# Sliding-window attention with a routed FFN on one core: transposes set between the long matmul groups, routing tail over seven steps, FFN weights in 0.5 MB pieces, row gathers two experts ahead

## The chip, the cores and the metric

The kernel runs on one core of one Trainium2 chip. The metric is the device time of one execution in microseconds (us); lower is better. The engines are TensorE (PE; its weight loads are shown apart as PEld), VectorE (DVE), ScalarE (ACT), GpSimd (POOL) and SyncE (SP), which here only issues DMAs.

## The reference

Two stages, for 8 batches of 576 tokens, 8 heads of 64:

```python
mask = (abs(pos_q - pos_k) <= 32) | is_global[q] | is_global[k]      # 8 global positions
attn = softmax(where(mask, q @ k.T / 8, -1e9))
x    = (attn @ v) as 4608 rows of 512
expert = argmax(x @ w_gate)                                          # 8 experts
gate   = softmax(x @ w_gate)[expert]
for e in range(8):
    out[rows of e] = gate * (relu(rows @ w1[e]) @ w2[e])             # 512 -> 1024 -> 512
```

## The kernel before

**Attention.** The loop runs over batches b = 0 to 7 and, in each, over six steps t. A step covers two window slices of all eight heads. `scores` (lines 383 and 396) puts the mask and q·k into one PSUM tile, one step ahead of use; `exps` (L403, ACT) takes the exponentials; `pvs` (L414) multiplies them with v, `zs` (L426) sums them, and `merge_x` and `merge_z` add both to the accumulators `xt` and `zt` (L444 on ACT, L447 and L449 on DVE). q and k of batch b+1 are transposed in steps 1 to 4 by `trans_qk` (L293 for k, copied by ACT L298; L291 for q, copied by DVE L295). The code runs in written order on each engine.

**The tail.** After a batch, `join` and `sum_globals` (POOL) finish `xt`, and the class `Tail` turns the batch into routed rows during the next batch's steps: `gate` (L500, copied by DVE L504), `logits` (L515, DVE to L523), `route1` (DVE and ACT), `ranks` (L580, L582), `route2` (DVE), `rows(i, f)` (L536, four transposes; DVE L537 scales the result into a 16-bit row buffer, `x16x` or a part of `wall`), and `scatter` (L613), six indirect DMAs on POOL that write rows into the slots of their experts in HBM (`xslot_scr`). All of `trans_qk`, `gate`, `logits`, `ranks` and `rows` take their PSUM tile from one pool of two buffers, in turn: the third must wait until DVE or ACT has copied the first.

**Weights.** `wall` holds the 16-bit weights of all experts (1 MB of 32-bit weights is one half of `w1` or `w2` of an expert). Those of experts 0 and 1 are loaded in batches 1 to 4 (two loads of 1 MB at t = 2 of each) and cast by ACT in the next batch's steps. The attention's buffers lie in the part of `wall` that belongs to later experts.

**Hand-over.** After batch 7 its own tail and that of the global rows run with nothing beside them, then the last scatters; then POOL computes an index constant (L755), DVE the gather indices and memsets (L784), and POOL issues the gathers (L774 and L775) of expert 0's four row blocks of 128.

**FFN.** For each expert, 32 matmuls `h` (L921) in eight groups, each with a relu in turn on ACT (L818) and DVE (L816); then 16 transposes of the next expert's rows (L798, copied by DVE L799); then 32 matmuls `yp` (L941) in four groups, each followed by `yout`: the gate is multiplied in by DVE (L807) or ACT (L805) into one of three `y` buffers, and an indirect DMA (L808, POOL) writes the rows to `out`. At the start of e the weights of e+3 are asked for in four loads of 1 MB, through two buffers `st`; each is cast by one instruction (POOL and DVE L638, ACT L636), which frees it for the next load. Rows of e+1 are gathered at the start of e. In e = 1 DVE also computes the overflow plan.

**Overflow.** Rows beyond an expert's first 512 run in blocks of 128, three to a chunk (nine blocks here): transposes `x`, matmuls `h` (L970), transposes `t` (L980), matmuls `y` (L989), all `yout` on ACT. Writes to `out` of this part are declared dependent on one another, so that each waits for the one before.

Of the kernel before, what the change touches and what calls it, by code (L numbers as in the profile page):

```python
# [38 lines left out]
NOV = 32  # L39
# [3 lines left out]
def kernel(  # L43
# [34 lines left out]
    qf = carve(128, H * 384, FP32)  # L78
    kf = carve(96, H * 384, FP32)
# [4 lines left out]
    stage = [carve(128, 2048, FP32) for _ in range(2)]  # L84
# [3 lines left out]
    def short(*shape):  # L88
        n = 1
        for d_ in shape:  # L90
            n *= d_
        a = early[0]
        early[0] = a + n
        assert early[0] <= 2048
        r = stage[1][:, a : a + n]
        return r.rearrange("p (a b) -> p a b", b=shape[1]) if len(shape) > 1 else r
# [19 lines left out]
    mask = carve(128, NSL * WE, FP16).rearrange("p (n w) -> p n w", n=NSL)  # L116

# [23 lines left out]
    ebasef = sb.tile([128, E], FP32, name="ebasef")  # L141
    gif4 = gidw.rearrange("p (g w) -> p g w", w=2)
# [201 lines left out]
    def routing_constants():  # L344
# [28 lines left out]
        nc.vector.tensor_copy(base[0], ebasef)  # L373
        nc.vector.scalar_tensor_tensor(out=tokg, in0=p8f[0:64], scalar=float(S), in1=gip[0:64], op0=ALU.mult, op1=ALU.add)
# [247 lines left out]
    pre = [(e, w, hf) for e in range(2) for w in range(2) for hf in range(2)]  # L622

    def wload(e, w, hf, st):
        if w == 0:
            src = moe_w1[e, 256 * hf : 256 * hf + 256].rearrange("(c p) f -> p c f", p=128)
            nc.sync.dma_start(out=st.rearrange("p (c f) -> p c f", c=2), in_=src)
        else:
            src = moe_w2[e, 512 * hf : 512 * hf + 512].rearrange("(c p) d -> p c d", p=128)
            nc.sync.dma_start(out=st.rearrange("p (c d) -> p c d", c=4), in_=src)  # L630

    def wcast(e, w, hf, st, eng, part=None):
        o = 4096 * w + 2048 * hf
        n, a = (2048, 0) if part is None else (1024, 1024 * part)
        if eng is nc.scalar:
            nc.scalar.activation(out=wall[:, e, o + a : o + a + n], in_=st[:, a : a + n], func=AF.Copy)  # L636
        else:
            eng.tensor_copy(wall[:, e, o + a : o + a + n], st[:, a : a + n])  # L638
# [7 lines left out]
    for b in range(B):  # L646
# [8 lines left out]
        if done is not None:  # L655
            done.scatter()
        casts = []
        for i, p_ in enumerate(staged):
            for hf in range(2):
                casts.append((p_, stage[i], hf))  # L660
        staged = [pre.pop(0) for _ in range(2)] if b >= 1 and pre else []
        for t in range(NT):
            n = NT * b + t
            tr = t - 1 if b + 1 < B and 1 <= t <= 4 else None
            if tr is not None:
                trans_qk(b + 1, tr, "k")
            if n + 1 < NT * B:
                sc = scores(*divmod(n + 1, NT))
                exps(n + 1, sc)
            pv = pvs(b, t)  # L670
            merge_x(b, t, pv)
            z = zs(b, t)
            merge_z(b, t, z)
            if tail is not None:
                if t == 0:
                    tail.gate(0)
                elif t == 1:
                    tail.logits(0)
                elif t == 2:
                    tail.logits(2)  # L680
                elif t == 3:
                    tail.rows(0, 1)
                elif t == 4:
                    tail.ranks()
                    tail.rows(1, 0)
                else:
                    tail.rows(1, 1)
            if tr is not None:
                trans_qk(b + 1, tr, "q")
            if tail is not None:  # L690
                if t == 0:
                    tail.gate(1)
                    tail.gate(2)
                elif t == 1:
                    tail.logits(1)
                elif t == 2:
                    tail.rows(0, 0)
                elif t == 3:
                    tail.route1()
                elif t == 5:  # L700
                    tail.route2()
                    tail.rows(2, 0)
                    tail.rows(2, 1)
            for _ in range(2 if t == 0 else 1):
                if casts:
                    p_, st_, hf = casts.pop(0)
                    wcast(*p_, st_, nc.scalar, hf)
            if t == 2:
                for i, p_ in enumerate(staged):
                    wload(*p_, stage[i])  # L710
        join(b, nc.gpsimd if b + 1 < B else nc.vector)
        sum_globals(b)
        done = tail
        tail = Tail(b)
    tg = Tail(B)
    done.scatter()
    tail.gate(0)
    tail.gate(1)
    tail.logits(0)
    tail.gate(2)  # L720
# [16 lines left out]
    tg.rows(0, 0)  # L737
    tail.scatter()
# [9 lines left out]
    fxr = ctx.enter_context(tc.tile_pool(name="fxr", bufs=10))  # L748
    fst = ctx.enter_context(tc.tile_pool(name="fst", bufs=2))
# [3 lines left out]

    ofs_i = fp.tile([128, 4], I32, name="ofs_i")
    nc.gpsimd.iota(ofs_i, pattern=[[128, 4]], base=0, channel_multiplier=1)  # L755
    ofs = fp.tile([128, 4], FP32, name="ofs")
    nc.vector.tensor_copy(ofs, ofs_i)
    cnt = fp.tile([128, E], FP32, name="cnt")
    nc.vector.tensor_tensor(out=cnt, in0=base[1], in1=ebasef, op=ALU.subtract)
    idf = fp.tile([128, E, 4], FP32, name="idf")  # L760
    cntb = cnt.rearrange("p (e o) -> p e o", o=1)
    ofsb = ofs.rearrange("p (o j) -> p o j", o=1).to_broadcast([128, E, 4])
    nc.vector.tensor_tensor(out=idf, in0=ofsb, in1=cntb.to_broadcast([128, E, 4]), op=ALU.is_ge)
    nc.vector.scalar_tensor_tensor(out=idf, in0=idf, scalar=BIG, in1=ofsb, op0=ALU.mult, op1=ALU.add)
    idx = fp.tile([128, E, 4], I32, name="idx")
    nc.vector.tensor_tensor(out=idx, in0=idf, in1=ebasef.rearrange("p (e o) -> p e o", o=1).to_broadcast([128, E, 4]), op=ALU.add)
# [15 lines left out]
    zr = [new_rows() for _ in range(10)]  # L782
    for x_ in zr:
        nc.vector.memset(x_, 0.0)  # L784
    del zr

    def gathers(e):
        r = []
        for j in range(4):
            xr = new_rows()  # L790
# [4 lines left out]
    def xtrans(xr, dst):  # L795
        ps = pst.tile([128, 4, 128], FP16, tag="tx", name="tx")
# [4 lines left out]
    def yout(ps, xr, eng, free=True):  # L801
        y = fy.tile([128, DM], FP32, tag="y", name="y")
# [17 lines left out]
    def wfetch(e):  # L820
        r = []
        for w in range(2):
            for hf in range(2):
                st = fst.tile([128, 2048], FP32, tag="st", name="st")
                wload(e, w, hf, st)
                r.append((e, w, hf, st))
        return r

    rows_e = gathers(0)
    wq = wfetch(2)  # L830
    xts = fp2.tile([128, 4, 512], FP16, tag="xts", name="xts")
    for j in range(4):
        xtrans(rows_e[j], xts[:, :, 128 * j : 128 * j + 128])
# [76 lines left out]
    NPRE = 12  # L910
    ovx = []
    for e in range(E):
        nxt = gathers(e + 1) if e + 1 < E else None
        plan = iter(overflow_plan()) if e == 1 else iter(())
        cast = wq
        wq = wfetch(e + 3) if e + 3 < E else []
        ht = fp2.tile([128, 8, 512], FP16, tag="ht", name="ht")
        for fb in range(8):
# [131 lines left out]
```

## Time and profile before

| | before |
|---|---|
| median of 3 runs | 548.08 us (547.62 to 551.95) |
| the profiled execution's own time | 549.16 us |
| its span | 547.3 us |
| mean granted TensorE clock | 0.891 of 2.4 GHz |
| PE busy | 395.0 us (72%) |
| DVE / ACT / POOL busy | 249.5 / 187.7 / 247.7 us |
| HBM read / written | 68.49 / 16.16 MB |

The span is what the profiler recorded, from the first to the last instruction. By the first instruction of each stage, the span divides so: start until 26.2 us; batch 0 until 53.5, batch 7 from 255.8 to 281.4, and the six between them, 33.7 us each on average; hand-over until 319.0; expert 0 until 336.3, then expert 1 from there, expert 6 from 455.0, expert 7 from 472.0; overflow from 486.6, its last matmul at 533.2. Shares of busy time over the whole span mix these stages.

### The profile page before, as it was taken

What the parts mean: (1) busy time and instruction counts of PE and PEld (TensorE: products, weight loads), DVE (VectorE), ACT (ScalarE), POOL (GpSimd) and SP (SyncE); (2) the same over time, 40 slices, a digit from 0 to 9 for tenths busy, and PEclk for the clock granted to TensorE, in tenths of its full rate; (3) what the DMA queues carried; (4) which work ended last, traced back from release to release, by engine and by line L of the source; (5) the groups of instructions that cost most, each with busy time, mean ns of one, the idle gap of its engine ahead of it and who ended that gap; (6) DMA issues with size and microseconds to landing.
All of it is one profiled execution on the core that took longest, in us unless ns stands there. A gap on an engine that the chain in (4) does not pass through costs nothing. (4 is left out here: it accounts for less than half of the span.)

```text
span 547.3 us, 15981 instructions
## 1 busy us (share of the span) xinstructions
PE 395.0 (72%) x6583; PEld 242.0 (44%) x6583; DVE 249.5 (46%) x682; ACT 187.7 (34%) x344; POOL 247.7 (45%) x383
## 2 busy tenths in 40 slices
PE   1478677777787877777966189678688768988880
PEld 1256455555655655555643144233233223444440
DVE  4433454455555455655677436716333243323220
ACT  3255342646446364443420013031221303223330
POOL 6640702807438074380625644443647466521211
PEclk9998986999888698998995579879888898999996
DMA  8898996895959757210102448667695954120100
GB/s 179 153 220 198 162 308 109 220 227 126 289 92 272 174 124 184 46 44 6 47 2 64 164 158 287 204 229 237 206 323 184 339 179 144 61 79 21 47 28 33
DMA packets 75613, 84.44 MB, mean 154 GB/s; under 512 B 44428, under 2 KB 57756, under 8 KB 75536
## 3 DMA queue, kind: packets, MB, share of 16 engines
q1 hardware_dynamic: 66384, 63.61, 44.7%
q0 software_dynamic: 8880, 19.37, 10.7%
q8 instruction: 54, 0.88, 0.7%
q10 hardware_dynamic: 272, 0.39, 0.3%
q14 instruction: 23, 0.19, 0.1%
HBM read 68.49 MB, written 16.16 MB: 155 GB/s over the span
## 5 line engine op out<-in xcount | busy, mean ns | idle before, releaser
L449 DVE TENSOR_TENSOR xt<-xt,pv 128x288 f32<-128x288 f32 x80 | 36.3, 454 | 95.2 <-ACT xt L444 94.8
L921 PE MATMUL h<-xts,wall 128*128 128x512 f16 x256 | 64.4, 410 | 10.3 <-ACT ht L818 9.7
L414 PE MATMUL pv<-wall 56*64 56x128 f32 x1536 | 63.5, 304 | 6.1 <-issue 5.0
L403 ACT ACTIVATE wall<-sc 128x1024 f32<-128x1024 f32 x48 | 49.1, 1023 | 54.1 <-PE sc L396 52.7
L941 PE MATMUL yp<-wall,ht 128*128 128x512 f16 x256 | 63.6, 410 | 4.7 <-DVE y L807 4.7
L808 POOL DMA_INDIRECT out_dram<-y,xr x32 | 31.6, 986 | 64.2 <-DVE y L807 40.5
L462 POOL TENSOR_TENSOR xt<-xt 128x144 f32<-128x144 f32 x14 | 7.1, 506 | 112.4 <-DVE xt L449 112.4
L414 PEld LDWEIGHTS pv<-wall 56*64 56x64 f32 x1536 | 50.2, 151 | 8.1 <-issue 6.4
L280 POOL CAST wall<-wall 96x768 f16<-96x768 f32 (+1 forms) x56 | 43.9, 823 | 9.8 <-DMA wall<-in_k_dram 7.0
L444 ACT ACTIVATE xt<-pv 128x224 f32<-128x224 f32 x96 | 34.2, 356 | 40.5 <-DVE xt L449 21.1
L921 PEld LDWEIGHTS <-wall 128*128 128x128 f16 x256 | 26.8, 105 | 47.3 <-issue 22.4
L816 DVE TENSOR_SCALAR ht<-h 128x512 f16<-128x512 f32 x32 | 22.1, 689 | 55.7 <-PE h L921 55.7
L536 PE MATMUL tr_x<-id,xt 128*108 128x128 f32 x192 | 34.1, 315 | 17.0 <-DVE tmp L523 6.4
L941 PEld LDWEIGHTS <-ht 128*128 128x128 f16 x256 | 26.4, 104 | 38.0 <-issue 12.9
L805 ACT ACTIVATE y<-yp,xr 128x512 f32<-128x512 f32 x16 | 11.0, 687 | 82.7 <-PE yp L941 64.4
L426 PE MATMUL z<-wall,onesel 56*32 56x128 f32 x1536 | 37.0, 301 | 3.0 <-issue 3.0
L775 POOL DMA_INDIRECT xr<-xslot_scr,idx x32 | 34.2, 1070 | 9.2 <-POOL xr L774 8.9
L818 ACT ACTIVATE ht<-h 128x512 f16<-128x512 f32 x32 | 18.4, 596 | 49.2 <-PE h L921 27.9
L798 PE MATMUL tx<-idh,xr 128*128 128x128 f16 x128 | 12.9, 238 | 30.4 <-DMA xr<-xslot_scr,idx 21.9
L536 PEld LDWEIGHTS tr_x<-id,xt 128*108 128x108 f32 x192 | 23.2, 150 | 24.5 <-issue 8.9
L298 ACT ACTIVATE kt<-tr_qk 128x576 f16<-128x576 f16 x32 | 20.7, 647 | 30.3 <-PE tr_qk L293 30.3
L396 PEld LDWEIGHTS <-kt 64*64 64x64 f16 x1536 | 26.6, 115 | 9.6 <-issue 4.9
(228 smaller groups left out, 691.2 us busy)
## 6 DMA issues: line engine op xcount, KB each, us to landing
st<-in_moe_w_dram SPq DMA_DIRECT2D x24, 1024.0 KB
wall<-in_k_dram SPq DMA_DIRECT2D x32, 288.0 KB
wall<-in_q_dram SPq DMA_DIRECT2D x32, 288.0 KB
wall<-in_v_dram SPq DMA_DIRECT2D x96, 96.0 KB
wall<-in_moe_w_dram SPq DMA_DIRECT2D x8, 1024.0 KB
wall<-vg SPq DMA_DIRECT2D x16, 96.0 KB
xr<-xslot_scr,idx POOLq DMA_INDIRECT x32, 2.9
out_dram<-y,xr POOLq DMA_INDIRECT x32, 2.8
```

Of the source, the lines that this page charges most:

```text
L280: eng.tensor_copy(o, i_)
L396: nc.tensor.matmul(out=o[:, NG:WE].rearrange("p (r a) -> p r a", r=R) if part == 0 else o[:, 0:NG], lhsT=kt[b % 2][rr, c, sl, :], rhs=rhs, ...
L403: nc.scalar.activation(out=e.rearrange("p r c w -> p r (c w)"), in_=sc[:, :, 0 : 4 * WE], func=AF.Exp, scale=0.125)
L414: nc.tensor.matmul(out=pv[64 * r : 64 * r + 64, f, c * WE : (c + 1) * WE], lhsT=vt[ff, t, 64 * h : 64 * h + 64], rhs=e[ff, r, c, :], start ...
L426: nc.tensor.matmul(out=z[32 * c : 32 * c + 32, f, 0:WE], lhsT=onesel[ff, r, :], rhs=e[ff, r, c, :], start=(r == 0), stop=(r == 1))
L444: nc.scalar.activation(out=new[i][0], in_=new[i][1], func=AF.Copy)
L449: nc.vector.tensor_tensor(out=d_, in0=d_, in1=s_, op=ALU.add)
L536: nc.tensor.transpose(out=ps[p, 128 * c : 128 * c + 128], in_=src, identity=id32)
L775: d_ = nc.gpsimd.indirect_dma_start(out=xr.bitcast(I16), out_offset=None, in_=xslot, in_offset=IndirectOffsetOnAxis(ap=ix, axis=0), bounds ...
L808: d_ = nc.gpsimd.indirect_dma_start(out=out, out_offset=IndirectOffsetOnAxis(ap=xr[:, DM : DM + 2].bitcast(I32), axis=0), in_=y, in_offset ...
L921: nc.tensor.matmul(out=ps, lhsT=w1v[:, e, c, 128 * fb : 128 * fb + 128], rhs=xts[:, c, :], start=(c == 0), stop=(c == 3))
L941: nc.tensor.matmul(out=ps, lhsT=ht[:, fc, 128 * j : 128 * j + 128], rhs=w2v[:, e, fc, :], start=(fc == 0), stop=(fc == 7))
```

## The change

Eleven edits in one rewrite:

- Attention: each step is written as k transposes (or a tail piece), scores, a tail piece, pv, q transposes (or a tail piece), z, a tail piece. Before, all of the tail pieces and the q transposes stood behind z.
- Tail: the last two `rows` and the scatters go to step 0 of the batch after; `sum_globals` moves ahead of the next batch's steps.
- Early weights come in pieces of 0.5 MB through four buffers in place of 1 MB through two, at the same step.
- The rows of experts 0 and 1 get eight buffers at the end of `wall` (`xr01`), set to zero by POOL before the last scatters; both are gathered right after these. The index constant and the indices are computed earlier.
- FFN weights come in 0.5 MB pieces through five buffers; a cast stands behind `h` groups 1, 3, 5 and 7 (ACT, DVE, ACT, DVE) and behind each `yout` (ACT, DVE, ACT, DVE), and asks for the next piece. POOL casts nothing.
- Rows are gathered two experts ahead, from 12 buffers (10 before).
- The overflow plan is drained within e = 1, overflow rows are gathered in e = 4 and 5 and, in the overflow, two chunks ahead; the transposes `x` run a chunk ahead, the first in expert 7. `yout` alternates ACT, DVE, ACT, and no write to `out` waits for another.

```diff
-NOV = 32
+NST = 5
+NOV = 33
...
-    stage = [carve(128, 2048, FP32) for _ in range(2)]
+    stage = [carve(128, 1024, FP32) for _ in range(4)]
...
+    xr01 = [wflat[:, 8 * 8192 - ROW * (i + 1) : 8 * 8192 - ROW * i] for i in range(8)]
...
-        if done is not None:
-            done.scatter()
...
+        if b:
+            sum_globals(b - 1)
...
             if tr is not None:
                 trans_qk(b + 1, tr, "k")
+            elif t == 0 and done is not None:
+                done.rows(2, 0)
+            elif t == 5 and tail is not None:
+                tail.ranks()
             if n + 1 < NT * B:
                 sc = scores(*divmod(n + 1, NT))
                 exps(n + 1, sc)
+            if t == 0 and done is not None:
+                done.rows(2, 1)
+                done.scatter()
+            elif tail is not None:
+                if t == 1:
+                    tail.gate(2)
...
             pv = pvs(b, t)
             merge_x(b, t, pv)
+            if tr is not None:
+                trans_qk(b + 1, tr, "q")
+            elif t == 0 and tail is not None:
+                tail.gate(0)
             z = zs(b, t)
             merge_z(b, t, z)
...
-            if tr is not None:
-                trans_qk(b + 1, tr, "q")
...
-        sum_globals(b)
...
+    for x_ in xr01:
+        nc.gpsimd.memset(x_, 0.0)
...
-        if free:
-            tc.declare_no_dep(d_.ins, group="out", reason="every token has a row of its own")
-            tc.add_to_no_dep_group("out", d_.ins)
+        tc.declare_no_dep(d_.ins, group="out", reason="every token has a row of its own")
+        tc.add_to_no_dep_group("out", d_.ins)
...
+    def fetch():
+        if pieces:
+            p_ = pieces.pop(0)
+            st = fst.tile([128, 1024], FP32, tag="st", name="st")
+            wload(*p_, st)
+            loaded.append((p_, st))
+
+    def castp(eng):
+        if loaded:
+            p_, st = loaded.pop(0)
+            wcast(*p_, st, eng)
+            fetch()
+
+    for _ in range(NST):
+        fetch()
+    rows_of = {0: gathers(0), 1: gathers(1)}
...
-        nxt = gathers(e + 1) if e + 1 < E else None
+        if e + 2 < E:
+            rows_of[e + 2] = gathers(e + 2)
...
-            for _ in range(5):
+            for _ in range(4):
                 next(plan, None)
-            if cast and fb in (1, 5):
-                wcast(*cast[fb // 4], nc.gpsimd if fb == 1 else nc.vector)
...
+            if fb % 2:
+                castp(nc.scalar if fb % 4 == 1 else nc.vector)
+        for _ in plan:
+            pass
...
-            if cast and j in (0, 2):
-                wcast(*cast[2 + j // 2], nc.scalar if j else nc.vector)
-            yout(ps, rows_e[j], "act" if j % 2 else "dve")
...
+            yout(ps, rows_of[e][j], "act" if j % 2 else "dve")
+            castp(nc.vector if j % 2 else nc.scalar)
...
+                for k_ in range(i + 6, min(i + 9, NOV)):
+                    gather(ovx[k_ % 9], ovi[:, k_ : k_ + 1])
+                b0.h()
+                b1.h()
+                b0.t()
+                b2.h()
+                b1.t()
+                b0.y("act")
+                for k_ in range(i + 3, min(i + 6, NOV)):
+                    xtrans(ovx[k_ % 9], oxt[k_ // 3 % 2][:, :, 128 * (k_ % 3) : 128 * (k_ % 3) + 128], take(pot))
+                b2.t()
+                b1.y("dve")
+                b2.y("act")
```

PE's row at the end of batch 1's step 5 and the step 0 behind it, before; the first is the last score matmul, `tr_x` are transposes of `rows`:

```order
L396 MATMUL sc<-qgt,kt_83 64x8
L414 MATMUL pv<-wall 64x128 x16
L426 MATMUL z<-wall,onesel 32x128 x16
L536 MATMUL tr_x<-id_85,xt_75 108x128 x12
L383 LDWEIGHTS id_87
L383 MATMUL sc<-wall,id_87 64x512
```

The same place after, with the end of step 0 as well (`tr_l` is `gate`):

```order
L405 MATMUL sc<-qgt,kt_83 64x8
L545 MATMUL tr_x<-id_85,xt_75 108x128 x4
L423 MATMUL pv<-wall 64x128 x16
L435 MATMUL z<-wall,onesel 32x128 x16
L545 MATMUL tr_x<-id_85,xt_75 108x128 x4
L392 LDWEIGHTS id_87
L392 MATMUL sc<-wall,id_87 64x512
...
L545 MATMUL tr_x<-id_85,xt_75 108x128 x4
L423 MATMUL pv<-wall 64x128 x16
L509 MATMUL tr_l<-xt_76,wgbd 32x216 x4
L435 MATMUL z<-wall,onesel 32x128 x16
L509 MATMUL tr_l<-xt_76,wgbd 32x216 x4
```

Twelve transposes in a row, through two buffers, are now three fours with a long matmul group between each two.

ACT's row of expert 0 before (L818 relu, L805 `yout`, L636 cast of 1 MB):

```order
L818 ACTIVATE ht<-h 128x512 x4
L805 ACTIVATE y<-yp,xr 128x512
L636 ACTIVATE wall<-st 128x2048
L805 ACTIVATE y<-yp,xr 128x512
```

And after (L833 relu, L821 `yout`, L643 cast of 0.5 MB):

```order
L833 ACTIVATE ht<-h 128x512
L643 ACTIVATE wall<-st 128x1024
L833 ACTIVATE ht<-h 128x512 x2
L643 ACTIVATE wall<-st 128x1024
L833 ACTIVATE ht<-h 128x512
L643 ACTIVATE wall<-st 128x1024
L821 ACTIVATE y<-yp,wall 128x512
L643 ACTIVATE wall<-st 128x1024
L821 ACTIVATE y<-yp,wall 128x512
```

One cast of 2048 columns between the two `yout` has become four of 1024, two of them among the relus.

POOL's row at the hand-over before (L613 scatters, L755 the index constant, L775 gathers of expert 0):

```order
L613 DMA xslot_scr<-wall,si 36864x516 x6
L613 DMA xslot_scr<-x16x,si 36864x516 x6
L613 DMA xslot_scr<-wall,si 36864x516
L755 IOTA ofs_i 128x4
L774 MEMSET xr 128x1
L775 DMA xr<-xslot_scr,idx 128x516
```

And after:

```order
L725 MEMSET wall 128x516 x8
L622 DMA xslot_scr<-wall,si 36864x516 x6
L622 DMA xslot_scr<-x16x,si 36864x516 x6
L622 DMA xslot_scr<-wall,si 36864x516
L784 MEMSET wall 128x1
L785 DMA wall<-xslot_scr,idx 128x516
```

Eight memsets stand ahead of the last scatters now, and the index constant no longer behind them.

## Rows read from the trace of the kernel before

**Rows 1.** Windows: us, busy of PE, PEld, DVE, ACT, POOL, clock, DMA share, GB/s.
```profile
53.50:191.70 138.20, 106.06 (x2835) 78.82 (x2831) 69.48 (x202) 66.78 (x132) 59.50 (x102) 0.88 0.82 198
191.70:255.80 64.10, 47.28 (x1425) 35.65 (x1421) 36.22 (x106) 30.99 (x64) 32.64 (x54) 0.96 0.38 86
255.80:281.40 25.60, 21.43 (x690) 15.94 (x683) 16.44 (x50) 11.66 (x27) 9.70 (x18) 0.97 0.10 27
319.00:455.00 136.00, 105.52 (x480) 46.76 (x480) 59.89 (x108) 32.09 (x41) 70.06 (x90) 0.89 0.70 234
420.00:440.00 20.00, 16.43 (x72) 7.07 (x72) 7.14 (x12) 5.45 (x7) 10.69 (x16) 0.91 0.86 287
455.00:472.00 17.00, 15.37 (x82) 7.29 (x81) 6.60 (x13) 3.86 (x7) 10.49 (x17) 0.99 0.24 76
472.00:486.60 14.60, 14.09 (x66) 6.13 (x64) 4.27 (x6) 3.77 (x7) 5.73 (x6) 1.00 0.25 94
486.60:533.20 46.60, 39.06 (x252) 20.41 (x252) 12.73 (x27) 16.37 (x27) 7.88 (x9) 1.00 0.11 40
```

**Rows 2.** PE's waits, 67 to 277 us: waiter, releaser: us in total, times, longest.
```profile
PE tr_lt L515 <- DVE tmp L523: 8.5, 6, 1.4
...
PE tr_qk L293 <- DVE qt L295: 1.8, 6, 0.3
```

**Rows 3.** Timeline, 214 to 219 us: start, busy us, instruction, idle before and its releaser.
```profile
214.14 1.07 PE L414 MATMUL pv<-wall 56*64 56x128 f32 x32
...
215.15 0.67 PE L426 MATMUL z<-wall,onesel 56*32 56x128 f32 x32
...
215.74 0.65 PE L536 MATMUL tr_x<-id,xt 128*108 128x128 f32 x4
...
216.23 0.50 PE L291 MATMUL tr_qk<-idh,wall 128*128 128x128 f16 x6
...
216.98 0.30 DVE L449 TENSOR_TENSOR zt<-zt,z 128x144 f32<-128x144 f32 x1
...
217.80 0.45 DVE L295 COPY qt<-tr_qk 128x576 f16<-128x576 f16 x1
217.93 0.41 PE L293 MATMUL tr_qk<-idh,wall 96*128 96x96 f16 x6 [1.20 <-DVE wall L537]
...
218.85 0.42 PE L414 MATMUL pv<-wall 56*64 56x128 f32 x8
```

**Rows 4.** Waits of the whole span: us in total, times, longest.
```profile
DVE xt L449 <- ACT xt L444: 94.8, 77, 4.2
...
DVE wall L638 <- DMA st<-in_moe_w_dram: 18.4, 6, 4.3
ACT wall L636 <- DMA st<-in_moe_w_dram: 15.4, 5, 4.7
ACT y L805 <- DMA out_dram<-y,xr: 15.1, 6, 4.3
```

**Rows 5.** Timeline, 444 to 454 us, expert 5: weight loads and their casts.
```profile
444.46 0.92 SPq L630 DMA_DIRECT2D st<-in_moe_w_dram  x2
...
449.93 1.23 DVE L638 CAST wall<-st 128x2048 f16<-128x2048 f32 x1 [4.31 <-DMA st<-in_moe_w_dram]
...
453.19 1.91 ACT L636 ACTIVATE wall<-st 128x2048 f16<-128x2048 f32 x1 [4.68 <-DMA st<-in_moe_w_dram]
```

**Rows 6.** Timeline, 307 to 317 us, the hand-over.
```profile
307.22 0.13 POOL L755 IOTA ofs_i<- 128x4 int32 x1 [0.92 <-DMA xslot_scr<-x16x,si]
...
309.49 1.06 POOL L775 DMA_INDIRECT xr<-xslot_scr,idx  x1 [0.75 <-POOL xr L774]
...
316.15 1.11 PE L798 MATMUL tx<-idh,xr 128*128 128x128 f16 x7 [12.55 <-DMA xr<-xslot_scr,idx]
```

**Rows 7.** Timeline, 529 to 547 us, the end.
```profile
529.61 3.62 PE L989 MATMUL oy<-wall,oht 128*128 x16
...
538.76 0.97 POOL L808 DMA_INDIRECT out_dram<-y,xo  x1 [4.33 <-DMA out_dram<-y,xo]
```

More of the change, by code (lines that the diff above doesn't have):

```diff
@@ L654 @@
                 load_qk(b + 2)
-        if done is not None:
-            done.scatter()
[L657 to L661, printed above, removed]
+        if b:
+            sum_globals(b - 1)
+        casts = list(zip(staged, stage))
+        staged = [pre.pop(0) for _ in range(4)] if b >= 1 and pre else []
         for t in range(NT):
@@ L669 @@
                 exps(n + 1, sc)
+            if t == 0 and done is not None:
[4 more added lines that the diff above has]
+                    tail.gate(2)
+                elif t == 2:
+                    tail.logits(1)
+                elif t == 3:
+                    tail.rows(0, 0)
+                elif t == 4:
+                    tail.rows(0, 1)
+                elif t == 5:
+                    tail.rows(1, 1)
             pv = pvs(b, t)
             merge_x(b, t, pv)
+            if tr is not None:
+                trans_qk(b + 1, tr, "q")
+            elif t == 0 and tail is not None:
+                tail.gate(0)
             z = zs(b, t)
@@ L675 @@
                 if t == 0:
-                    tail.gate(0)
+                    tail.gate(1)
                 elif t == 1:
@@ L681 @@
                 elif t == 3:
-                    tail.rows(0, 1)
+                    tail.route1()
                 elif t == 4:
-                    tail.ranks()
                     tail.rows(1, 0)
                 else:
-                    tail.rows(1, 1)
-            if tr is not None:
-                trans_qk(b + 1, tr, "q")
[L690 to L700, printed above, removed]
                     tail.route2()
-                    tail.rows(2, 0)
-                    tail.rows(2, 1)
             for _ in range(2 if t == 0 else 1):
                 if casts:
-                    p_, st_, hf = casts.pop(0)
-                    wcast(*p_, st_, nc.scalar, hf)
+                    p_, st_ = casts.pop(0)
+                    wcast(*p_, st_, nc.scalar)
             if t == 2:
-                for i, p_ in enumerate(staged):
-                    wload(*p_, stage[i])
+                for p_, st_ in zip(staged, stage):
+                    wload(*p_, st_)
         join(b, nc.gpsimd if b + 1 < B else nc.vector)
-        sum_globals(b)
         done = tail
         tail = Tail(b)
+    sum_globals(B - 1)
+    for x_ in xr01:
+        nc.gpsimd.memset(x_, 0.0)
     tg = Tail(B)
-    done.scatter()
     tail.gate(0)
+    done.rows(2, 0)
     tail.gate(1)
     tail.logits(0)
+    done.rows(2, 1)
+    done.scatter()
     tail.gate(2)
@@ L780, in gather @@
                 mybir.DependencyClass.Sync, mybir.DependencyReason.DATA), reason="slots of all tokens")
[L782 to L785, printed above, removed]
+    fresh = [12]
     def gathers(e):
@@ L789, in gathers @@
         for j in range(4):
-            xr = new_rows()
+            if e < 2:
+                xr = xr01[4 * e + j]
+            else:
+                xr = new_rows()
+                if fresh[0]:
+                    fresh[0] -= 1
+                    nc.vector.memset(xr, 0.0)
             gather(xr, idx[:, e, j : j + 1])
@@ L818, in relu @@
             nc.scalar.activation(out=dst, in_=ps, func=AF.Relu)
[L820 to L830, printed above, removed]
+    pieces = [(e, w, i) for e in range(2, E) for w in range(2) for i in range(4)]
+    loaded = []
+    def fetch():
[12 more added lines that the diff above has]
+    rows_of = {0: gathers(0), 1: gathers(1)}
     xts = fp2.tile([128, 4, 512], FP16, tag="xts", name="xts")
     for j in range(4):
-        xtrans(rows_e[j], xts[:, :, 128 * j : 128 * j + 128])
+        xtrans(rows_of[0][j], xts[:, :, 128 * j : 128 * j + 128])
     nbm_i = fp.tile([128, NOV], I32, name="nbm_i")
@@ L991, in y @@
                                  start=(fc == 0), stop=(fc == 7))
-            yout(ps, self.xr, "act", free=False)
+            yout(ps, self.xr, eng, take(oy))
     nov = nc.values_load(novi[0:1, 0:1], min_val=0, max_val=NOV)
```

145 lines of the change are left out of this document (69 added, 76 removed).

## The prediction

> **What bounds the kernel now.** I read the windows by stage first, since one share for the whole span says nothing about where time can go. In batches 1 to 4 (the first of [rows 1]) PE is busy 106.1 of 138.2 us and the DMA engines 0.82 of the time; the reader is to see that both are near full, neither is full, and that 0.82 x 138.2 / 4 = 28.3 us of transfers per batch is a floor there for any change of PE's order. In batches 5 and 6 (the second) DMA falls to 0.38 and PE is still busy only 47.3 of 64.1 us: something else holds PE. The FFN from expert 0 to 5 (the fourth) has PE at 105.5 of 136.0 us and DMA at 0.70, while expert 6, which waits for no weights, takes 17.0 us and expert 7 takes 14.6 (the sixth and seventh); so weights cost the first six 22.7 - 17 = about 6 us each. The overflow (the eighth) keeps PE busy 39.1 of 46.6 us.
>
> Second, PE's waits in the attention [rows 2]: ten rows, of which the first and last are shown, sum to 43.3 us over 6.2 batches, 7 us a batch, and every one is a transpose of some kind waiting for DVE to empty one of the two PSUM buffers. The timeline [rows 3] shows why: after z, a rows piece and a q transpose go out back to back (215.74, 216.23), both buffers are then full, DVE is still at the merges, and the next k transpose starts at 217.93 after 1.20 us of idling; nothing of scores can pass it. Third, waits that end on a DMA [rows 4]: casts wait for weight loads 18.4 + 15.4 us, ACT's `y` for written rows 15.1 us.
>
> **The change part by part.** The sum is made against the profiled execution, 549.16 us (span 547.3), 1.1 above the median.
>
> *A, attention.* The same instructions are issued; their order changes, and with it which wait is last. New step, by [rows 3]: pv ends at 215.15. DVE reaches the q copy where it now does the z merge, at 216.98, and ends 0.45 later, 2.28 after pv's end; PE has by then done q transposes, z and a tail piece (0.50 + 0.6 + 0.49). Then 0.06 to see the semaphore, k transposes and scores 0.92 (217.93 to 218.85), a tail piece 0.49 (215.74 to 216.23), pv 1.01 (214.14 to 215.15): 4.76 us. Step 5 has ranks for k and no q (4.7), step 0 carries a rows piece more (5.1): 28.8 a batch for 33.7. What is late next is DVE's merge chain, with the q copy behind it. In batches 1 to 4 the transfers' 28.3 stand right below this and rarely fit perfectly, so I take 30 for all six: 6 x 3.7 = 22. Batch 7 has no q or k transposes; PE is busy 21.4 of its 25.6 us (the third of [rows 1]), and I take 3 of the 4.2. Together **-25**. Bounds: -35 if every batch runs at the transfers' floor, 28.5, and batch 7 loses all idling; -10 if only batches 5 to 7 gain. Scatters, moved to step 0, run past POOL's casts of q and k of a later batch; POOL is busy 59.5 of 138.2 us, which covers them. Nothing is queued behind `sum_globals` but POOL's casts.
>
> *B, hand-over.* The gathers of expert 0 waited behind the index constant (307.22), the indices and DVE's memsets until 309.49 [rows 6]; without these they go at about 307.1, and the transposes, 6.7 us after the first gather (316.15), with them: -2.4. On the other side eight memsets on POOL stand ahead of the last scatters; POOL's time for these is not in the trace. The indices and ten such memsets on DVE lie within the 2.3 us from 307.22 to 309.49, so some 2 us is one end, and nothing the other, if the scatters wait longer for DVE's rows anyway. Five weight pieces (2.6 MB) instead of two (2 MB) compete with the gathers, 0.6 MB at 334 GB/s, 1.8 us at worst. I take **-1.5**, bounds -5 and +2.
>
> *C, FFN.* PE's own work is 14.1 us in expert 7 [rows 1] and with 16 transposes and their copies 15.4 to 17.0 (expert 6): call 16.5. The transfers of an expert with weights are 4.19 MB weights, 0.53 gathered and 1.05 written, 5.77 MB; from 420 to 440 us 287 GB/s moved at a share of 0.86 (the fifth of [rows 1]), so 334 at full share, 17.3 us, and at 94% 18.4. So transfers set it: 6 x 18.4 = 110.4 for 136.0. The deeper queue is what gives that share: before, two pieces were out, and when both were out the cast waited (casts at 449.93 and 453.19, after 4.31 and 4.68 us of idling, for loads issued at 444.46 [rows 5]). Casts grow from 4 to 8, in all the same columns; POOL's part goes to ACT and DVE, which are busy 32.1 and 59.9 of 136.0 us and have room, and four of 1024 columns delay a relu by half a cast, some 1 us, while three PSUM buffers are in turn. Expert 6: 0.5 less. Expert 7 takes the first overflow transposes, +1. Together -25.6 - 0.5 + 1 = **-25**. Bounds: -34 with PE's floor of 16.5 and no transfer in the way (136 - 99 = 37, less the start); -4 where pieces come no faster than now.
>
> *D, overflow.* With transposes a chunk ahead and gathers two ahead, a chunk should come near PE's busy time: 39.1 for 46.6 us, of which I take 7. At the end three writes wait in turn: 529.61 to 533.2 the last matmuls, the last write issued at 538.76 after 4.33 us on the one before [rows 7]. Free, it is issued about 534.4, -4.3. Together **-11**, bounds -7 and -14 (no idling at all, and the first chunk's transposes gone to expert 7).
>
> Sum: -25 - 1.5 - 25 - 11 = -62.5; 549.2 - 62.5 - 1.1 = **485.5**.
>
> **The rivals.**
>
> *Slower: pieces whose fixed part shows.* From [rows 5], the first 1 MB cast started 5.5 us after its issue, the second 3.26 later: 3.26 us moves 1 MB, and 2.2 are fixed. Were the fixed part to be paid for each piece in turn, 0.5 MB takes 2.2 + 1.6 = 3.8 us, 8 of them 30.7 us an expert, 12.3 more than forecast, six times: 485.5 + 74 = **559**. It is slower than before from 3.6 us a piece (62.5 / 48 = 1.3 above the 2.3 that I take). Against it: the second load's fixed part lay under the first, and now five are out. Chance 0.04. The Trainium skill, "DMA: Bandwidth & Descriptors", section "Measured (HBM→SBUF, 128 partitions, SWDGE, issued from GpSimd)", has a rule against this change: to batch transfers to 1 MiB or more for 75% of peak. By its figures, 0.95 us for 64 KB and 6.15 for 1 MB, 0.5 MB would be about 3.4 us, an estimate, 27 us an expert, and the sum 537; no run here shows it yet, and the 287 GB/s of the trace, with two out, says that such times overlap.
>
> *Attention hardly moves.* DVE's merge chain, which I make the new bound, may already be the old one behind the transposes, and batches 1 to 4 may be held by transfers (0.82). Then A is -10: **500**. For it: 94.8 us of DVE's idling end on ACT's half of the merge [rows 4]; against: 7 us a batch of PE's waits end on DVE's other work. Chance 0.15.
>
> *FFN held by written rows.* Still three `y` buffers, whose writes take up to 4.3 us to free them [rows 4], and writes compete with five loads in place of two. If an expert stays at 21.3, C is -8: **502**. Chance 0.15.
>
> *Better.* Both at their floors, A -35 and C -34, some 19 more: **466**. Chance 0.15.
>
> **How the numbers follow.** The forecast has 0.5, the rivals 0.04, 0.15, 0.15 and 0.15, and 0.01 is left. The range goes from 460 (the better case with B's and D's ends) to 512 (one of the two weak cases, with D and B at their weak ends), and leaves out the slower case and the weak cases together. A measurement of this kernel can tell about 1%, 5.5 us, from no change. Only the slower rival and some double failures end above 543: faster 0.94, same 0.02, slower 0.04.
>
> **What would show it.** A: batches 1 to 6 of 29 to 31 us each, PE's waits on DVE below 3 us a batch, the q copy ending last. B: the first gather issued right behind the last scatter, expert 0's transposes about 1.5 us sooner after it. C: experts 0 to 5 18 to 19 us apart, DMA share above 0.9, few waits of casts. D: chunks of about 13 us, the last three writes issued within 5 us. I am wrong if DMA's share in the FFN stays near 0.7 with casts waiting (pieces too small), if `y` waits for writes grow, or if the attention's batches stay above 32 us with DVE or ACT between PE's steps.

## The result and the profile after

The changed kernel takes **502.9 us** (median of 4, 501.6 to 504.14) where the kernel before took 548.92 in the same comparison: ratio 0.9154, 95% interval 0.9108 to 0.92. Forecast were 485.5 us, range 460 to 512. The profiled execution has a span of 502.4 us for 547.3, 44.9 less; 62.5 were forecast.

In the second and third group of experiments (from the fifth kernel on) the chip ran the kernel before in 580 and 586 us, and batches 2 to 6 of every kernel traced there took some 35 to 39 us each; those kernels are therefore compared with the control of their group and by stages, never with 502.9.

The page of the profile after begins:

```profile
span 502.4 us, 16112 instructions
PE 383.6 (76%) x6595; PEld 233.1 (46%) x6595; DVE 248.3 (49%) x696; ACT 199.6 (40%) x359; POOL 246.5 (49%) x391
```

PE has the same work and is 11.4 us less busy: it ran at a higher clock. Where, the windows by stage tell (columns as in [rows 1]): batches 1 to 4, batches 5 and 6, batch 7, hand-over, experts 0 to 5, expert 6, expert 7, overflow. The first three begin at the first score matmul of a batch's step 0, some 4 to 5 us later in a batch than those of [rows 1]; the list by batch further down uses this mark on both sides.

```profile
58.60:187.70 129.10, 104.93 (x2835) 74.85 (x2832) 69.72 (x202) 67.52 (x131) 59.06 (x101) 0.91 0.83 205
187.70:243.60 55.90, 48.28 (x1423) 34.61 (x1422) 36.07 (x106) 31.90 (x65) 32.71 (x54) 1.00 0.44 98
243.60:265.50 21.90, 19.50 (x622) 13.65 (x621) 15.80 (x49) 10.40 (x25) 9.73 (x18) 1.00 0.11 31
265.50:304.10 38.60, 15.32 (x101) 8.74 (x102) 19.54 (x74) 1.35 (x7) 28.29 (x47) 0.63 0.37 123
304.10:417.10 113.00, 95.13 (x480) 44.35 (x481) 59.19 (x129) 43.48 (x59) 59.49 (x81) 0.96 0.81 275
417.10:434.30 17.20, 15.15 (x81) 7.23 (x80) 5.68 (x10) 3.55 (x6) 6.17 (x7) 1.00 0.25 97
434.30:450.10 15.80, 14.83 (x78) 6.98 (x77) 5.36 (x9) 4.04 (x7) 4.43 (x5) 1.00 0.14 53
450.10:491.90 41.80, 38.86 (x252) 20.35 (x251) 14.99 (x30) 14.60 (x24) 18.92 (x28) 1.00 0.15 50
```

Against [rows 1]: the 480 matmul records of experts 0 to 5 took 95.1 us for 105.5 at a granted clock of 0.96 for 0.89, so 10.4 of the 23.0 us gained there are the same matmuls at more of the higher clock level, and 12.6 are idling that went. The whole difference follows; the overflow begins with its first transposes before, and after, where these stand in expert 7, with its first `h` (by that mark it begins at 487.6 before):

| stage | before | after | difference | forecast |
|---|---|---|---|---|
| start to the end of the last z (attention) | 281.4 | 265.4 | -16.0 | -25 |
| hand-over, to the first `h` | 37.6 | 38.7 | +1.1 | -1.5 |
| experts 0 to 5 | 136.0 | 113.0 | -23.0 | -25.6 |
| experts 6 and 7 | 31.6 | 33.0 | +1.4 | +0.5 |
| overflow, to its last matmul | 46.6 | 41.8 | -4.8 | -7 |
| from there to the end | 14.1 | 10.5 | -3.6 | -4.3 |

Within the attention, from the first score matmul of step 0 to that of the next batch: 28.4, 37.2, 33.1, 33.2, 35.4, 32.6 and 32.4 us for batches 0 to 6 before, and 29.6, 33.4, 32.5, 29.7, 33.6, 28.1 and 27.7 after; from there to the end of batch 7, 20.2 before and 21.9 after.

PE's waits from 67 to 243 us, the ones that answer to [rows 2]:

```profile
PE sc L405 <- issue: 8.2, 5, 4.3
PE tr_qk L300 <- DVE qt L302: 6.9, 9, 0.9
PE pv L423 <- issue: 3.9, 4, 1.8
PE tr_p L589 <- DVE qt L302: 3.7, 5, 1.0
...
PE tr_lt L524 <- issue: 1.8, 1, 1.8
...
PE z L435 <- issue: 1.3, 2, 0.8
```

The waits of transposes on DVE, 43.3 us in ten rows before, are 16.1 now: 5.0 on the tail's work, the rest the k transposes' (and ranks') wait for the q copy. Beside these stand 15.2 us in which the row names no releaser (`issue`), in twelve waits; before, these were five, 4.3 us. The step that the forecast worked out, in batch 5 (timeline; z, ACT and DVE's merges, q copy, next k transposes):

```profile
195.81 0.90 PE L435 MATMUL z<-wall,onesel 56*32 56x128 f32 x32
...
196.90 0.46 DVE L458 TENSOR_TENSOR xt<-xt,pv 128x288 f32<-128x288 f32 x1 [0.42 <-ACT xt L453]
...
197.28 0.45 DVE L302 COPY qt<-tr_qk 128x576 f16<-128x576 f16 x1
...
197.78 0.41 PE L300 MATMUL tr_qk<-idh,wall 96*128 96x96 f16 x6 [0.71 <-DVE qt L302]
```

From pv's end (195.4) to the k transposes it is 2.3 us, where 2.28 + 0.06 were forecast, and the three steps there, from score to score, are 4.9, 4.9 and 4.6 us for 4.76: DVE's merge chain with the q copy behind it is the new bound, as forecast, where transfers leave PE alone.

### The profile page after: what moved, and what is told of

It reads as the page before. It is cut to its first block, busy times and chain, and to the rows that moved or that the text cites. A ratio compares the mean times of both kernels' runs of the same rounds, so it can differ in the third digit from the quotient of the medians.

```text
span 502.4 us, 16112 instructions
## 1 busy us (share of the span) xinstructions
PE 383.6 (76%) x6595; PEld 233.1 (46%) x6595; DVE 248.3 (49%) x696; ACT 199.6 (40%) x359; POOL 246.5 (49%) x391
## 5 line engine op out<-in xcount | busy, mean ns | idle before, releaser
L943 PE MATMUL h<-xts,wall 128*128 128x512 f16 x256 | 62.0, 399 | 10.4 <-ACT ht L833 9.8
L423 PE MATMUL pv<-wall 56*64 56x128 f32 x1536 | 61.2, 294 | 6.5 <-issue 5.4
L458 DVE TENSOR_TENSOR xt<-xt,pv 128x288 f32<-128x288 f32 x80 | 36.3, 454 | 59.4 <-ACT xt L453 58.9
L412 ACT ACTIVATE wall<-sc 128x1024 f32<-128x1024 f32 x48 | 49.1, 1024 | 34.1 <-PE sc L405 32.5
L969 PE MATMUL yp<-wall,ht 128*128 128x512 f16 x256 | 56.6, 379 | 0.0
L423 PEld LDWEIGHTS pv<-wall 56*64 56x64 f32 x1536 | 47.0, 143 | 17.1 <-issue 13.3
L943 PEld LDWEIGHTS <-wall 128*128 128x128 f16 x256 | 25.9, 102 | 45.1 <-issue 18.4
L824 POOL DMA_INDIRECT out_dram<-y,xr x24 | 25.0, 1041 | 41.4 <-DVE y L823 26.7
L833 ACT ACTIVATE ht<-h 128x512 f16<-128x512 f32 x32 | 19.0, 596 | 37.9 <-PE h L943 37.9
L405 PEld LDWEIGHTS <-kt 64*64 64x64 f16 x1536 | 25.1, 111 | 14.8 <-issue 10.1
L821 ACT ACTIVATE y<-yp,xr 128x512 f32<-128x512 f32 x12 | 8.2, 687 | 57.5 <-PE yp L969 37.1
L300 PE MATMUL tr_qk<-idh,wall 96*128 96x96 f16 x192 | 14.9, 219 | 19.7 <-ACT wall L285 11.0
L622 POOL DMA_INDIRECT xslot_scr<-wall,si x25 | 24.9, 995 | 8.7 <-issue 5.1
L785 POOL DMA_INDIRECT xr<-xslot_scr,idx x24 | 25.5, 1062 | 7.0 <-POOL xr L784 6.7
L622 POOL DMA_INDIRECT xslot_scr<-x16x,si x24 | 23.9, 994 | 9.0 <-issue 4.3
```

Source lines behind the costliest of these rows:

```text
L412: nc.scalar.activation(out=e.rearrange("p r c w -> p r (c w)"), in_=sc[:, :, 0 : 4 * WE], func=AF.Exp, scale=0.125)
L423: nc.tensor.matmul(out=pv[64 * r : 64 * r + 64, f, c * WE : (c + 1) * WE], lhsT=vt[ff, t, 64 * h : 64 * h + 64], rhs=e[ff, r, c, :], start ...
L458: nc.vector.tensor_tensor(out=d_, in0=d_, in1=s_, op=ALU.add)
L622: d_ = nc.gpsimd.indirect_dma_start(out=xslot, out_offset=IndirectOffsetOnAxis(ap=self.si[p, j : j + 1], axis=0), in_=self.x16[p, j, :].bi ...
L785: d_ = nc.gpsimd.indirect_dma_start(out=xr.bitcast(I16), out_offset=None, in_=xslot, in_offset=IndirectOffsetOnAxis(ap=ix, axis=0), bounds ...
L824: d_ = nc.gpsimd.indirect_dma_start(out=out, out_offset=IndirectOffsetOnAxis(ap=xr[:, DM : DM + 2].bitcast(I32), axis=0), in_=y, in_offset ...
```

## The experiments

**Attention alone, and all but the attention.** The first puts the new loop into the kernel before, the second the old loop into the changed one.

```diff
# first: before, with
...
+            if tr is not None:
+                trans_qk(b + 1, tr, "q")
+            elif t == 0 and tail is not None:
+                tail.gate(0)
             z = zs(b, t)
# second: after, with
-            if t == 0 and done is not None:
-                done.rows(2, 1)
-                done.scatter()
...
+            if tr is not None:
+                trans_qk(b + 1, tr, "q")
```

> The kernel before with the attention's new order alone (tail over seven steps, transposes between the long groups); early weights still in 1 MB pieces, hand-over gathers, FFN and overflow as before. If the stages' gains are separate, as the two traces read (the attention's last pv ends 15.9 us sooner), 548.9 - 16 = 533. If the 0.5 MB early pieces carry a part of that (batches 1 to 4 gained 9.9 of it, 5 and 6 gained 9.1), the order alone gives 9: 540.

> The changed kernel with the attention's old order put back; everything else as changed. Separate gains: 502.9 + 16 = 519. If the two halves help each other (smaller early pieces need the new order or the reverse), 525 or more; if the new order costs the hand-over what it gained, 511.

Measured: 530.8 us (528.55 to 533.18) and 518.6 (516.58 to 522.42), ratios to before 0.9772 (0.9646 to 0.9899) and 0.9568 (0.9396 to 0.9739), where before itself spread from 539.86 to 556.94 in this group. The changed kernel with its memsets moved (below) had 0.9271 there, so the two parts add up to the whole within that spread. By the traces: spans 531.4 and 517.3, that is -15.9 and -30.0 from 547.3, together -45.9 for -44.9. In the first the attention ends at 266.9 (265.4 in the changed kernel) with batches 5 and 6 at 28.4 and 27.7; its FFN takes 167.0 us. In the second the attention ends at 281.3 and the FFN takes 144.6. The two halves are separate; the smaller early pieces carry at most 1.5 us.

**Overflow gathers behind the written rows.**

```diff
-        if e in (4, 5):
-            ... three gathers ...
         for j in range(4):
             ... yp, yout, castp ...
+        if e in (4, 5):
+            ... three gathers ...
```

> The changed kernel with the three overflow gathers of experts 4 and 5 behind the four written row blocks instead of ahead of them on POOL. Theory: expert 5 took 21.0 us against 17.5 for expert 4 because the writes stood behind these gathers and ACT waited 8.0 us for a y buffer with a relu behind it; then 3.5 us there and 1.4 in expert 6 go: 498. Rival: transfers set the pace of these experts anyway, 503.

What it was after stands in the timeline of the changed kernel, at the end of expert 4:

```profile
392.35 1.00 POOL L785 DMA_INDIRECT xo<-xslot_scr,ovi  x1 [0.27 <-POOL xo L784]
...
395.38 1.04 POOL L824 DMA_INDIRECT out_dram<-y,xr  x1 [2.04 <-issue]
...
400.62 0.69 ACT L821 ACTIVATE y<-yp,xr 128x512 f32<-128x512 f32 x1 [8.00 <-DMA out_dram<-y,xr]
401.20 0.59 ACT L833 ACTIVATE ht<-h 128x512 f16<-128x512 f32 x1
...
401.84 2.72 PE L943 MATMUL h<-xts,wall 128*128 128x512 f16 x6 [4.85 <-ACT ht L833]
```

The first of expert 4's `y` was ready at 390.0 and its write issued at 395.38, behind the last gather; ACT's fourth `y` waits 8.00 us for that buffer, a relu stands behind it, and PE waits 4.85 us. The window of expert 5 in the changed kernel, then in this experiment (columns as above):

```profile
394.24:417.13 22.89, 16.77 (x82) 7.59 (x80) 8.96 (x17) 7.33 (x10) 12.97 (x19) 0.93 0.63 201
```

```profile
397.59:415.05 17.46, 15.13 (x81) 7.21 (x80) 8.91 (x18) 7.32 (x10) 11.02 (x17) 1.00 0.72 258
```

5.4 us went in this expert, where 3.5 were expected, and 6.8 in the FFN (139.2 for 146.0). The whole kernel took 500.3 us (495.6 to 504.44), ratio 0.9165 with an interval from 0.8942 to 0.9387: its attention, unchanged code, ended at 271.2 for 265.4 in the profiled run, which hides the gain. The rival falls for this expert: the `y` buffers held it, not the transfers.

**Memsets out of the hand-over.** POOL's eight memsets go to step 0 of batch 7.

```diff
+                if b == B - 1:
+                    for x_ in xr01:
+                        nc.gpsimd.memset(x_, 0.0)
```

> The changed kernel with POOL's eight memsets moved from ahead of the last scatters to step 0 of batch 7. Theory: the last scatters wait for DVE's last rows (ready at 288.2, last scatter issued at 289.24), so only 1 us goes: 502. Rival: POOL is back to back from the memsets to the last scatter, so all 3.9 us go: 499.

502.97 us (501.49 to 504.81); hand-over 38.4 us for 38.7. The memsets cost nothing: the last scatters wait for DVE's rows.

**Fewer bytes on the way, and pieces of 1 MB.** Two buffers of 0.5 MB; and two of 1 MB, cast in halves.

```diff
-NST = 5
+NST = 2
# second one, as well
-            st = fst.tile([128, 1024], FP32, tag="st", name="st")
+            st = fst.tile([128, 2048], FP32, tag="st", name="st")
...
-            fetch()
+            if p_[2] % 2:
+                fetch()
```

> The changed kernel with two weight buffers of 0.5 MB instead of five. By the slower rival's arithmetic of the prediction a piece costs 2.2 fixed and 1.6 moving; with two out and each refetched only after its cast, an expert takes at least 4 x (2.2 + 3.3) = 22 us and some waiting for its cast's turn, 25 to 28: 503 + 6 x 8 = 550. If the many small casts spread over the expert are what helped, and not the bytes on the way, 503 to 510.

> The changed kernel with weight loads of 1 MB through two buffers (as before), each cast in two halves at the new places, the next load asked for after the second half. If the bytes on the way count (2.1 MB now, 2.6 with five pieces), an expert takes 18 to 19: 505 to 512. If the finer release of buffers counts, experts go back towards the 23 us of before: 530.

564.6 us and 544.0, where the changed kernel itself, in the group after, took 543.8 at almost the same time for before (586 and 580). By stages: windows of experts 0 to 5 with two buffers of 0.5 MB, with two of 1 MB, and of the control.

```profile
340.60:476.00 135.40, 105.14 (x481) 47.72 (x482) 60.20 (x128) 44.79 (x59) 60.63 (x88) 0.88 0.76 244
```

```profile
341.00:458.40 117.40, 97.42 (x481) 44.95 (x482) 59.56 (x129) 44.84 (x59) 60.85 (x84) 0.94 0.79 270
```

```profile
343.70:455.80 112.10, 94.88 (x481) 44.41 (x482) 59.33 (x129) 43.48 (x59) 60.33 (x83) 0.96 0.81 277
```

And what the casts of the first wait for:

```profile
ACT wall L643 <- DMA st<-in_moe_w_dram: 53.4, 18, 4.7
...
DVE wall L645 <- DMA st<-in_moe_w_dram: 24.8, 16, 3.6
```

Two pieces on the way give 22.6 us an expert (22 to 28 were expected), 2.8 us a piece; five give 18.7, 2.3 a piece; 2.1 MB in two pieces gives 19.6 (18 to 19 expected). At the same size, then, five on the way for two are worth 3.9 us an expert. Between five of 0.5 MB and two of 1 MB it is 0.9 us; there size and bytes on the way (2.6 and 2.1 MB) both differ, so the size by itself has no price here. The rule of the Trainium skill on batching to 1 MiB ("DMA: Bandwidth & Descriptors", "Measured (HBM→SBUF, 128 partitions, SWDGE, issued from GpSimd)") would have favoured the larger piece; with two on the way the traces agree (19.6 for 22.6), but five smaller ones beat two larger (18.7 for 19.6).

**Rows gathered one expert ahead.**

```diff
-    rows_of = {0: gathers(0), 1: gathers(1)}
+    rows_of = {0: gathers(0)}
...
-        if e + 2 < E:
-            rows_of[e + 2] = gathers(e + 2)
+        if e + 1 < E:
+            rows_of[e + 1] = gathers(e + 1)
```

> The changed kernel itself, as the control of this call: 503 where the chip runs before at 549, experts 5 and 1 the longest (22.9 and 19.4 us).

> The changed kernel with rows gathered one expert ahead instead of two (the gathers of expert 1 go at the start of expert 0, not before it). If gathering ahead hides what transposes waited for, each expert from 1 on waits for rows as in the kernel before (21.9 us in ten waits there, 12.6 of it in the hand-over): 505 to 511. If one ahead is enough once POOL casts nothing: 503, or 501 with the hand-over's four fewer gathers beside the first rows.

Control 543.8 us (543.3 to 544.36), one ahead **569.5** (569.16 to 571.14), ratios to before 0.9291 and 0.973. FFN 171.3 us for 145.1: with five pieces on the way and rows one expert ahead, as in the kernel before (168.6 to its first overflow `h`), all of the FFN's gain is gone. Timeline of an expert with one ahead (gathers on POOL, transposes on PE):

```profile
413.08 1.37 POOL L785 DMA_INDIRECT xr<-xslot_scr,idx  x1 [0.27 <-POOL xr L784]
...
418.09 1.00 POOL L785 DMA_INDIRECT xr<-xslot_scr,idx  x1 [0.27 <-POOL xr L784]
418.37 0.40 PE L813 MATMUL tx<-idh,xr 128*128 128x128 f16 x4 [1.91 <-DMA xr<-xslot_scr,idx]
...
420.51 0.40 PE L813 MATMUL tx<-idh,xr 128*128 128x128 f16 x4 [1.75 <-DMA xr<-xslot_scr,idx]
...
424.26 0.61 PE L813 MATMUL tx<-idh,xr 128*128 128x128 f16 x4 [1.71 <-DMA xr<-xslot_scr,idx]
```

POOL comes to the gathers only behind the last written rows of the expert before; the first rows are there 5.3 us after their issue, the last 6.2, and the expert's `h` groups are done by 416.5. Rows arrive 8 us too late, and PE's clock falls with its idling: the window of that expert, and of the same expert in the control:

```profile
409.24:433.05 23.81, 17.41 (x81) 7.75 (x80) 9.34 (x18) 7.32 (x10) 9.66 (x13) 0.86 0.70 241
```

```profile
398.10:415.90 17.80, 15.14 (x81) 7.22 (x80) 8.09 (x14) 7.33 (x10) 9.68 (x13) 1.00 0.94 326
```

Both expectations fall: 2 to 8 us were named, and 25.7 were measured.

**Early weights left out, and spread.** Once the loads of batches 2 to 4 are left out (run twice; experts 0 and 1 then compute with the weights of batch 1's loads), once the four pieces go one a step.

```diff
# left out
-            if t == 2:
+            if t == 2 and b == 1:
# spread
-            if t == 2:
-                for p_, st_ in zip(staged, stage):
-                    wload(*p_, st_)
+            if staged and 1 <= t <= 4:
+                wload(*staged[t - 1], stage[t - 1])
```

> The changed kernel without the early weight loads of batches 2 to 4 (12 of 16 pieces, 6.3 MB; the casts stay and read what batch 1 loaded, so the output of expert 0 and 1 is not the reference's). Theory: batches 2 to 4 took 32.5, 29.7 and 33.6 us in the changed kernel against 28.1 and 27.7 of batches 5 and 6, because transfers fill the DMA engines and PE stands still there for no releaser that the trace names (4.3, 1.8 and 1.8 us), at the lower clock after; without these loads they take 28 to 29 each, 503 - 11 = 492. Rival: the tail's DVE work or q, k and v loads hold them, and nothing changes: 503.

> The changed kernel with the four early pieces of a batch asked for one a step, in steps 1 to 4, instead of all four in step 2. If PE's stalls come from the burst (2.1 MB at once), batches 1 to 4 lose some 5 us together: 498. If it is the bytes of a batch, whenever they come, nothing changes: 503.

> The changed kernel without the early weight loads of batches 2 to 4 (the output of experts 0 and 1 is not the reference's), again: the chip of the first trial held every attention batch at 35 us or more, that of before too, and could not tell. Theory: batches 2 to 4, 32.5, 29.7 and 33.6 us in the changed kernel, fall to 28 to 29: 11 us less than the control. Rival: they stay, 0 to 3 us less.

545.0, 545.1 and 546.4 us, not told apart from the control's 543.8; the 11 us of the theory did not come. Batches 2 to 4: 35.9, 35.4, 38.0 and, again, 35.6, 36.3, 35.6 without the loads; 38.2, 35.3, 35.1 spread; 38.3, 36.3, 35.5 in the control. From 91 to 202 us the DMA share was 0.55 without them for 0.70, at the same clock of 0.86. Leaving the loads out gave nothing there; but batches 5 and 6, without any weights, took 35.5 us and more too, so something else held every batch, and these runs cannot say what held batches 1 to 4 where batches 5 and 6 took 28. The trace of the changed kernel says more (part A below).

**A version with what was learnt.** Overflow gathers behind the written rows, and the overflow plan's DVE work over two experts.

```diff
...
-            for _ in range(4):
+            for _ in range(2):
                 next(plan, None)
...
-        for _ in plan:
-            pass
+        if e == 2:
+            for _ in plan:
+                pass
...
```

> The changed kernel with the overflow gathers behind the written row blocks, and the overflow plan's DVE work spread over experts 1 and 2 instead of 1 alone. The first gave 5.4 us in expert 5 and 6.8 over the FFN where it was run by itself. Theory for the second: expert 1 took 19.4 to 21.1 us in all runs against 16.2 to 17.4 for expert 2, because plan operations stand between DVE's relus; spread, the two together take 2 us less: 503 - 7 - 2 = 494. Rival: the plan's time is only moved to expert 2: 496.

543.1 us (540.28 to 544.97) for the control's 543.8: not told apart, where 7 to 9 us less were expected. Expert 5 took 17.3 us for 22.3, expert 1 20.5 for 19.4 (the plan was not what made it long), expert 6 20.2 for 17.2 at a clock of 0.92 in its window; FFN 141.8 for 145.1. No run here shows a version that beats the changed kernel as a whole.

## Why the prediction was right, and where it was off

Direction and range held: every part but the hand-over gained. The size was 17.6 us too large, from four terms, and one term came near by luck (C).

*A, -16.0 for -25.* The mechanism held where it could be read alone: batches 5 and 6 gained 4.5 and 4.7 us each, 3.7 taken, with the step at its forecast length. Batch 0, which the sum left out, got 1.2 us longer. Two steps failed. "I take 3 of the 4.2" in batch 7: it got 1.7 us longer. Around its last step, which has no scores, only ranks stand between two rows pieces, and the second waits as long for DVE to empty the first one's buffer:

```profile
260.65 0.65 PE L545 MATMUL tr_x<-id,xt 128*108 128x128 f32 x4
...
262.42 0.68 DVE L546 TENSOR_TENSOR wall<-tr_x,rz 108x512 f16<-108x512 f32 x1
...
263.16 0.65 PE L545 MATMUL tr_x<-id,xt 128*108 128x128 f32 x4 [1.70 <-DVE wall L546]
```

And "I take 30 for all six": batches 1 to 4 took 32.3 on average, gaining 9.7 together for 14.8. There PE stands without a releaser and goes on at the lower clock; the largest case, in batch 1 (timeline, then windows around it, columns as above):

```profile
82.74 0.21 PE L405 MATMUL sc<-qgt,kt 64*64 64x8 f16 x2 [4.33 <-issue]
...
84.06 1.99 PE L423 MATMUL pv<-wall 56*64 56x128 f32 x32
```

```profile
78.00:84.00 6.00, 1.67 (x40) 1.20 (x32) 1.98 (x9) 1.54 (x3) 0.00 (x0) 0.74 1.04 341
84.00:88.50 4.50, 4.50 (x82) 3.48 (x81) 2.23 (x6) 1.24 (x4) 0.00 (x0) 0.58 0.98 173
```

The DMA engines were full (341 GB/s) while PE stood, and a pv group that takes 1.10 us at the full clock took 1.99 behind it.

What PE waits for can be read from the trace: its own next instructions. The page of the profile has a queue for these, of 54 packets, 16 KB each:

```profile
q8 instruction: 54, 0.88, 0.8%
```

Number PE's records in order of time, weight loads and semaphore instructions included: all twelve waits on `issue` from 67 to 243 us stand at a number that is 193 more than a multiple of 256, and so do the five before. At each, PE goes on 1.2 to 1.6 us after a packet of that queue has ended; for the wait of 4.33 us the packet ran from 80.14 to 81.42, and PE went on at 82.74. Ten of the twelve, 13.9 us, lie in batches 1 to 4, for 4.3 us before; without these 9.6 us more, the four batches would have gained about 4.8 us each, like batches 5 and 6. So the step failed by a term that it put at nothing. Why the packets come late is less sure. The one behind the longest wait began 5.7 us after PE had entered the 256 instructions before, with the DMA share at 1.10; from 222 to 254 us, at a share of 0.11, they began after 0.3 to 1.7 us. That fits transfers in their way; no run took these away from batch 1, and without the weight loads of batches 2 to 4 such waits of up to 3.3 us were left, at a share of 1.09 from other loads.

*B, +1.1 for -1.5.* The first gather went 27.2 us after the attention's end for 28.1, a gain of 0.9 and not 2.4. One step that failed is "without these they go at about 307.1": the gather goes 3.4 us after the issue of the last scatter in all twelve kernels with the new hand-over, 4.1 before, so the index work had cost it 0.7 us; the 2.34 us of POOL's idling below name no releaser. The other is "and the transposes, 6.7 us after the first gather (316.15), with them". The first block was there 6.5 us after its gather, but the other three waited on:

```profile
292.63 1.05 POOL L785 DMA_INDIRECT wall<-xslot_scr,idx  x1 [2.34 <-issue]
...
299.12 0.61 PE L813 MATMUL tx<-idh,wall 128*128 128x128 f16 x4 [11.64 <-DMA wall<-xslot_scr,idx]
...
301.70 1.84 PE L813 MATMUL tx<-idh,wall 128*128 128x128 f16 x12 [1.97 <-DMA wall<-xslot_scr,idx]
...
304.10 1.44 PE L943 MATMUL h<-xts,wall 128*128 128x512 f16 x3 [0.56 <-POOL e8i L876]
```

From first transpose to first `h` it is 5.0 us, where [rows 6] and the first `h` at 319.0 give 2.9. It is not the four extra gathers (4.8 with one ahead). From the first gather to the first `h` it goes with the weights on the way: 10.8 to 11.5 us in the ten kernels with five pieces of 0.5 MB, 9.9 with two of 1 MB, 8.0 with two of 0.5 MB, and 9.5 before. So the competing pieces cost 1.6 to 2.0 us, what the prediction had as "1.8 us at worst", and they took back all that the earlier gather gave.

*C, -21.6 for -25.* Experts 0 to 5 came to 113.0 us for 110.4, the nearest term, but by luck, and its reason failed. Experts 2 to 4 took 17.2 to 17.4 us, below the 18.4; experts 0, 1 and 5, at 18.9, 19.4 and 22.9, made up for it. And expert 6, which loads no weights, takes 17.2 too, as long as experts 3 and 4 at DMA shares of 0.95 and 0.96, so it is not shown that transfers set the pace there. The casts wait for no load any more (33.8 us before [rows 4]). "The deeper queue is what gives that share" failed: the FFN takes 171.3 us with the queue of five and rows one ahead, 150.0 with rows two ahead and two pieces of 1 MB, as much on the way as before, and 145.1 with both; the kernel before, to the same mark, took 168.6. So rows two ahead carry most of the gain and the deeper queue some 5 us, and only with the rows; a queue shallower than before, two pieces of 0.5 MB, loses it all (167.8). The casts' new places, none on POOL, were in all of these runs and not tried apart. The prediction named the row gathers in the change and gave them no price. The rival "FFN held by written rows" was true of one expert: 5.4 us in expert 5, by three gathers on POOL ahead of the writes; moved, that went. Expert 7 took 15.8 us with the first overflow transposes, +1.2 for +1.

*D, -8.4 for -11.* A chunk takes 14.2 us for the 13 taken: PE is busy 13, and the second and third begin with some 1.1 us in which their weight loads wait for nothing shown. The last write left at 492.90, 1.0 us after the last matmul; no write waits for another, as forecast.

```profile
464.15 3.23 PEld L1003 LDWEIGHTS <-oxt 128*128 128x128 f16 x16 [1.12 <-issue]
464.26 3.61 PE L1003 MATMUL poh<-wall,oxt 128*128 x16 [0.74 <-issue]
```

The slower rival, 559 us from 3.8 us a piece, fell: a piece costs 2.3 us with five on the way, 2.8 with two.

## What to carry to other kernels

Where a stage waits for two kinds of transfers, price each wait as if the other were cured: the deeper queue gave nothing with rows gathered one expert ahead (171.3 us, 168.6 before) and 4.9 with rows two ahead; the earlier gathers gave 26.2 under it. Look along the queue of the engine that issues a transfer: three gathers ahead of four writes on POOL cost 5.4 us through a buffer that ACT needed and a relu behind it. And a floor taken from one kind of batch (4.76 us a step without weight loads) is not the pace of batches that also move weights; take those apart in the sum. Where an engine waits for nothing that is named, count the instructions between such waits and look whether a packet of the instruction queue ended just before.

## What the runs showed of the hardware

In the later groups PE went through its instructions one or two at a time for a stretch of each batch from 2 on, in batches without weight loads too: some 0.7 us apart, with nothing named that it waits for. From the control, batch 5 (timeline):

```profile
219.06 0.10 PEld L392 LDWEIGHTS <-id 64*64 64x64 f16 x1 [0.61 <-issue]
...
220.49 0.15 PEld L405 LDWEIGHTS <-kt 64*64 64x64 f16 x4 [1.30 <-issue]
...
221.21 0.12 PEld L405 LDWEIGHTS <-kt 64*64 64x64 f16 x1 [0.57 <-issue]
...
221.92 0.54 PEld L405 LDWEIGHTS <-kt 64*64 64x64 f16 x25 [0.59 <-issue]
...
222.03 0.26 ACT L453 ACTIVATE zt<-z 128x112 f32<-128x112 f32 x1 [6.18 <-remote]
```

Batches 5 and 6 took 71.7 us there for 55.9 at a clock of 0.88 for 1.00, while the FFN, with far fewer PE instructions in a microsecond, took 145.1 for 146.0. The Trainium skill ("Runtime: NRT & Kernel Launch", "Instruction fetch mechanics") says that each engine's instructions are fetched by DMA in blocks of 16 KiB, 256 instructions, mostly hidden. The trace of the changed kernel agrees on the block, and shows where the fetch is not hidden: the twelve waits of part A, 15.2 us. The stretches of the later groups are another matter: their stops stand at no such place, and ACT stands at the same time, so their cause stays open.
